# Linear attention and a mixture of adapters in one kernel: filler products moved to listed places, and VectorE adds x for seven groups

## The chip, the cores and the metric

The kernel runs on one NeuronCore of one Trainium2 chip. The metric is the device time of one execution in microseconds. Thirteen executions of the kernel before were timed: median 109.11 us, lowest 107.42, highest 112.18.

Five engines work side by side, each through its own list of instructions in order: TensorE (PE; its weight loads are shown as PEld), VectorE (DVE), ScalarE (ACT), GpSimd (POOL) and SyncE (SP). In this kernel GpSimd and SyncE mostly issue transfers.

## What is computed

Two stages, cut to what matters:

```
r_q, r_k = relu(q), relu(k)                      # 8 batches, 8 heads, 576 rows, 64 columns
q_p = concat(r_q * cos, r_q * sin);  k_p likewise # cos, sin depend on the row
kv  = k_p^T v ;  z = sum over rows of k_p
x   = (q_p kv) / (q_p z + 1e-6)                   # then seen as 4608 rows of 512
logits = x @ w_gate                               # 8 experts
w   = softmax over the two largest logits of a row, zero elsewhere
out = x + sum over experts e of  w[e] * (x @ A[e]) @ B[e]      # A: 512x16, B: 16x512
```

The last line matters here: the output is x plus the adapters' part d.

## The kernel before

**Groups.** The 4608 output rows are 36 groups of 128 rows. The groups of batches 0 to 5 are called by batch and number, (0,0) to (5,8); those of batches 6 and 7 are done in pairs and called (7,0) to (7,8). The chain of one batch is: load k, v and q (cast to bf16 on the way); relu of k (L417); v times cos and sin (`vscale`, L427; VectorE takes 0.67 us for half a batch and 1.27 for a whole one, ScalarE does the same in nine pieces); the products k^T v (`kv_mm`, L439) into a PSUM tile `pnd`; and two copies of those to SBUF as `BD` (`kv_evac`, L454). The chain of one group is: transposes of q (L533) and a relu copy (L539) and the tangent factor (`qt_tan`, L545); the numerator and denominator products (`num_mm`, L562) into a `pnd` tile; a reciprocal (L589) and the division (`x_xt`, L594), which gives x as `xt` in bf16; transposes of x (L603) and their copy; the products with A and the gate (L616); the routing weights on VectorE (L630 to L665); a transpose of the weighted result (L674) and its copy; and last the output products.

**The output products.** For each group `dx_mm` (L682) puts two products of 512 columns in one PSUM bank `ps`: x by the identity matrix (L685), then the weighted result by B on top of it (L687). `osb` (L690) copies the sum to SBUF, on ScalarE (L241) or VectorE (L243), and a store carries it out.

**PSUM.** There are two `pnd` tiles of two banks each (128 x 2 x 512 f32) and four `ps` banks. Of each bank of a `pnd` tile the work uses columns 0 to 259; columns 260 to 511 are unused.

**Fillers.** Eighteen products of a constant tile `warm` open TensorE's list, and eighteen more follow later (`pe_warm`, L298). In addition `pe_more` (L305) puts products of 252 columns into the unused columns of the *first* bank of the `pnd` tile that the step has just written: six behind each of the four half-batch `kv` steps of batches 0 and 1 (L501) and four behind each of the `num` steps of the first five groups (L742), 44 in all:

```
    def pe_more(t, n):
        for _ in range(n):
            nc.tensor.matmul(out=t[:, 0, 4 * W:512], lhsT=warm[:, 0:128], rhs=warm[:, 4 * W:512], ...)
```

W is 65. The reader of a `pnd` tile takes both banks in one instruction, columns 0 to 259 of each, so its address range covers those filler columns of the first bank.

**Order.** All work is 594 steps. `ORDER` (L20) gives the order in which they are emitted, and so the order on each engine; `CHOICE` (L48) says which engine takes a step that has alternatives; `SLOTS` (L66) gives the buffer numbers. The costs and due times in the `pl.add` calls fed the planning that made these lists; nothing is planned when the kernel is built. `HOLD` (L79) makes four stores wait for an earlier issue. Loads go out on GpSimd's queue, the first k through SyncE; each load on GpSimd's queue also waits for the transfer that was issued eight before it. Most stores stand in SyncE's list, the rest behind the loads in GpSimd's.

Of the kernel before, what the change touches and what calls it, by code (L numbers as in the profile page):

```python
# [20 lines left out]
    26, 19, 32, 16, 20, 51, 15, 27, 14, 18, 0, 17, 1, 36, 2, 9, 29, 3, 12, 10, 52, 28, 33, 13, 31, 35, 4, 30, 11, 7,  # L21
    34, 5, 46, 37, 21, 6, 54, 50, 55, 38, 45, 39, 23, 8, 40, 44, 61, 114, 115, 41, 116, 22, 60, 125, 117, 42, 124, 43,
    126, 134, 70, 121, 127, 118, 53, 62, 122, 154, 119, 135, 120, 155, 145, 71, 144, 49, 123, 128, 69, 48, 299, 24,
    156, 131, 129, 47, 130, 298, 136, 132, 301, 133, 56, 146, 137, 79, 65, 302, 300, 57, 25, 78, 303, 58, 59, 355, 64,
    147, 141, 356, 138, 357, 360, 142, 358, 63, 80, 139, 140, 143, 304, 151, 359, 361, 305, 152, 66, 362, 88, 306, 73,
    373, 68, 74, 67, 363, 364, 148, 89, 160, 374, 161, 149, 375, 150, 171, 162, 170, 153, 307, 157, 172, 163, 308,
    376, 378, 164, 309, 158, 173, 87, 181, 159, 200, 377, 180, 201, 191, 165, 379, 166, 190, 182, 167, 380, 311, 192,
    174, 202, 183, 96, 381, 310, 72, 168, 175, 365, 169, 97, 369, 176, 177, 382, 178, 385, 193, 366, 75, 312, 179,
    107, 82, 386, 314, 393, 370, 77, 76, 313, 367, 315, 394, 187, 395, 398, 396, 184, 397, 81, 98, 83, 412, 185, 399,
    188, 186, 316, 189, 194, 400, 317, 203, 195, 413, 106, 196, 216, 217, 414, 417, 368, 197, 204, 415, 318, 416, 218,  # L30
    319, 320, 198, 418, 206, 199, 207, 321, 401, 205, 84, 105, 419, 402, 208, 219, 322, 387, 91, 383, 86, 323, 388,
    430, 209, 85, 392, 405, 384, 92, 210, 324, 420, 213, 211, 421, 406, 246, 403, 431, 247, 212, 226, 372, 227, 404,
    432, 236, 435, 90, 228, 237, 450, 433, 214, 248, 238, 93, 451, 215, 434, 452, 410, 407, 99, 95, 220, 453, 94, 455,
    229, 422, 408, 223, 221, 239, 454, 423, 424, 222, 426, 425, 390, 436, 224, 230, 437, 427, 326, 225, 438, 325, 231,
    439, 328, 456, 232, 329, 327, 233, 457, 444, 234, 330, 101, 429, 458, 440, 240, 459, 441, 235, 469, 445, 241, 446,
    100, 331, 332, 243, 333, 447, 262, 470, 263, 242, 253, 264, 252, 244, 272, 474, 471, 245, 273, 254, 102, 472, 265,
    473, 274, 255, 464, 462, 475, 110, 103, 389, 460, 463, 249, 428, 465, 476, 334, 335, 461, 250, 109, 477, 442, 478,
    466, 283, 336, 282, 487, 251, 443, 108, 479, 284, 337, 448, 488, 111, 275, 338, 492, 489, 285, 480, 483, 113, 411,
    490, 481, 104, 391, 491, 507, 112, 493, 494, 482, 256, 508, 484, 495, 509, 292, 257, 510, 486, 485, 496, 258, 259,
    293, 512, 501, 511, 260, 499, 261, 502, 266, 371, 513, 294, 500, 497, 514, 340, 506, 505, 267, 269, 268, 498, 467,  # L40
    515, 339, 270, 503, 342, 271, 341, 276, 504, 343, 344, 277, 279, 468, 516, 278, 526, 280, 281, 345, 286, 346, 527,
    347, 528, 287, 517, 529, 531, 288, 348, 449, 289, 530, 518, 543, 532, 290, 533, 349, 544, 519, 350, 291, 521, 520,
    548, 534, 545, 295, 546, 522, 535, 524, 523, 351, 547, 296, 538, 549, 352, 525, 550, 536, 409, 539, 297, 540, 537,
    551, 560, 552, 541, 353, 561, 555, 542, 354, 562, 565, 557, 563, 564, 553, 556, 566, 567, 579, 558, 554, 568, 569,
    580, 570, 559, 581, 584, 571, 582, 574, 583, 575, 572, 585, 589, 586, 573, 576, 577, 587, 588, 578, 590, 592, 591,
    593,
]
CHOICE = [  # L48
    0, 0, 0, 0, 0, 0, 0, 0, 0, 0, 0, 0, 0, 0, 0, 0, 0, 0, 0, 0, 0, 0, 0, 0, 0, 1, 0, 0, 0, 0, 0, 0, 0, 0, 0, 1, 0, 0,
    0, 0, 0, 0, 0, 1, 0, 0, 0, 0, 0, 1, 0, 0, 0, 1, 0, 1, 0, 0, 1, 0, 0, 0, 0, 0, 1, 0, 0, 0, 0, 0, 0, 0, 1, 0, 0, 0,  # L50
    0, 1, 0, 0, 0, 0, 0, 1, 0, 0, 0, 0, 0, 0, 0, 0, 0, 0, 0, 0, 0, 0, 0, 0, 0, 0, 0, 0, 1, 0, 0, 0, 0, 0, 0, 0, 0, 0,
# [4 lines left out]
    0, 0, 0, 0, 0, 0, 0, 0, 0, 0, 0, 0, 0, 0, 0, 0, 0, 0, 0, 0, 0, 0, 0, 0, 0, 0, 0, 0, 0, 0, 0, 0, 0, 0, 0, 0, 0, 1,  # L56
    0, 0, 0, 0, 0, 0, 0, 0, 0, 0, 0, 0, 0, 0, 1, 0, 0, 0, 0, 0, 0, 0, 0, 0, 0, 0, 0, 0, 0, 0, 0, 0, 0, 0, 0, 0, 0, 0,
    0, 1, 0, 0, 0, 0, 0, 0, 0, 0, 0, 0, 0, 0, 0, 0, 0, 0, 0, 0, 0, 0, 0, 0, 0, 0, 0, 0, 0, 0, 1, 0, 0, 0, 0, 0, 0, 0,
    0, 0, 1, 0, 0, 0, 0, 0, 0, 0, 1, 0, 1, 0, 0, 0, 0, 0, 0, 0, 0, 0, 0, 0, 0, 0, 1, 0, 0, 0, 1, 0, 0, 0, 0, 0, 0, 0,
    0, 0, 0, 0, 0, 0, 0, 0, 0, 0, 0, 1, 0, 0, 0, 0, 0, 0, 0, 0, 0, 0, 0, 0, 0, 0, 0, 0, 0, 1, 0, 0, 0, 0, 0, 0, 0, 0,  # L60
    0, 0, 0, 0, 0, 0, 0, 0, 0, 0, 0, 0, 0, 0, 0, 0, 0, 0, 0, 0, 0, 0, 0, 0, 0, 0, 0, 0, 0, 0, 1, 0, 0, 0, 0, 0, 0, 0,
    0, 0, 0, 0, 0, 0, 0, 0, 0, 0, 0, 0, 1, 0, 0, 0, 0, 0, 0, 0, 0, 0, 1, 0, 0, 0, 0, 0, 1, 0, 1, 1, 0, 0, 0, 0, 0, 0,
    0, 0, 0, 0, 0, 0, 0, 0, 0, 0, 0, 0, 0, 0, 0, 0, 0, 0, 0, 0, 1, 0, 0, 0, 0, 0, 1, 0, 0, 0, 0, 0, 0, 0, 0, 0, 0, 0,
    0, 0, 0, 1, 0, 0, 1, 1, 0, 0, 0, 0, 0, 0, 0, 0, 0, 0, 1, 0, 0, 0, 0, 0,
]
SLOTS = [  # L66
    2, 1, 0, 3, 0, 1, 0, 0, 0, 0, 0, 0, 1, 1, 1, 1, 0, 1, 2, 2, 2, 2, 1, 2, 3, 3, 3, 0, 0, 3, 0, 0, 4, 1, 0, 0, 1, 1,
    0, 2, 1, 1, 2, 2, 2, 0, 0, 2, 3, 3, 1, 1, 1, 3, 0, 0, 0, 1, 0, 1, 0, 1, 2, 1, 0, 2, 2, 1, 1, 3, 1, 2, 0, 2, 4, 1,
    0, 5, 0, 4, 1, 2, 6, 0, 1, 7, 3, 3, 1, 0, 8, 1, 0, 0, 2, 9, 1, 1, 10, 0, 1, 0, 0, 11, 1, 2, 12, 1, 2, 0, 1, 13, 1,
    0, 14, 3, 3, 0, 2, 15, 0, 0, 0, 0, 4, 1, 1, 2, 2, 1, 1, 2, 4, 0, 0, 1, 0, 0, 0, 1, 5, 1, 2, 3, 3, 4, 0, 0, 7, 1,  # L70
    1, 6, 1, 3, 0, 2, 8, 1, 0, 9, 1, 2, 1, 1, 10, 2, 0, 0, 2, 11, 1, 0, 14, 3, 1, 0, 1, 12, 1, 2, 2, 0, 4, 0, 0, 0, 1,
    1, 15, 0, 3, 0, 2, 13, 1, 0, 4, 1, 2, 0, 1, 5, 2, 0, 3, 1, 0, 2, 3, 3, 0, 0, 2, 1, 2, 2, 1, 3, 1, 0, 3, 1, 1, 2,
    0, 0, 2, 3, 1, 1, 0, 0, 2, 2, 1, 1, 0, 3, 0, 0, 3, 2, 2, 1, 1, 0, 0, 0, 3, 0, 2, 2, 1, 3, 2, 1, 1, 1, 1, 1, 0, 3,
    1, 3, 0, 0, 0, 0, 0, 0, 0, 4, 3, 3, 3, 1, 1, 1, 0, 1, 1, 5, 3, 1, 2, 0, 0, 0, 2, 0, 3, 6, 1, 2, 0, 1, 1, 1, 0, 1,
    0, 0, 2, 3, 1, 0, 0, 0, 3, 1, 2, 1, 1, 0, 3, 1, 1, 1, 3, 0, 1, 5, 3, 0, 2, 0, 0, 0, 3, 1, 3, 3, 3, 2, 2, 1, 1, 1,
    0, 0, 2, 1, 0, 3, 1, 0, 0, 0, 1, 1, 2, 2, 1, 3, 0, 1, 1, 1, 0, 0, 2, 5, 3, 1, 0, 0, 0, 1, 1, 0, 0,
# [3 lines left out]
    (371, 429), (389, 106), (411, 372), (449, 506),  # L80
# [65 lines left out]
def kernel(  # L146
# [86 lines left out]
    def pF(u):  # L233
        return pS[S_(u)][:, :]
# [70 lines left out]
    def pe_more(t, n):  # L305
        for _ in range(n):
            nc.tensor.matmul(out=t[:, 0, 4 * W:512], lhsT=warm[:, 0:128], rhs=warm[:, 4 * W:512], start=True, stop=True,
                             skip_group_check=True)
# [130 lines left out]
    def kv_mm(aa, uk, uvv, up, more=0):  # L439
        def f():  # L440
            kt, vt, pt = tK[S_(uk)], tVV[S_(uvv)], pND[S_(up)]
            for a in aa:
                for j in range(J):
                    for par in range(2):
                        for hh in range(2):
                            r = slice(64 * par, 64 * par + 64)
                            nc.tensor.matmul(  # L447
                                out=pt[64 * hh:64 * hh + 64, par, a * 2 * W:(a + 1) * 2 * W], lhsT=kt[r, 2 * a + hh, j, :],
                                rhs=vt[r, 2 * a + hh, j, :].rearrange("p (c w) -> p c w", c=2)[:, :, 0:W],
                                start=(j == 0), stop=(j == J - 1), skip_group_check=True)  # L450
            pe_more(pt, more)
        return f
# [20 lines left out]
    for b in range(B):  # L473
# [25 lines left out]
        for ai, aa in enumerate([[0], [1]] if b in HALF else [[0, 1]]):  # L499
            more = 6 if b in HALF else 0  # L500
            pl.add("kv", one("PE", 0.02 + 0.58 * len(aa) + 0.105 * more, kv_mm(aa, uk, uvv, upk, more)), d + 9 + ai,  # L501
                   needs=[("k", b, a) for a in aa] + [("vv", b, a, cs) for a in aa for cs in range(2)] + VCOLS,
                   makes=[("kvp", b, a) for a in aa], uses=[uk, uvv, upk, ubd], ins=72 * len(aa) + 2 * more)
# [58 lines left out]
    def num_mm(m, gs, uqt, und, more):  # L562
        g = gs[m]

        def f():
# [15 lines left out]
            pe_more(nd, more)  # L581
# [100 lines left out]
    def dx_mm(udx, uxt, uzt, i, part):  # L682
        def f():
            if part != 1:
                nc.tensor.matmul(out=pF(udx), lhsT=ident, rhs=tXT[S_(uxt)], start=True, stop=False)  # L685
            if part != 0:
# [167 lines left out]
```

## Time and profile before

| | |
|---|---|
| median of 13 executions | 109.11 us (107.42 to 112.18) |
| the profiled execution: its own time | 108.23 us |
| its span from first to last instruction | 106.4 us |
| loads (28.85 MB read from HBM) | end near 72 us |
| last instruction of a compute engine | ends at 102.5 us; then the last store |

| what, on which line | engine | count | from start to the next start, or mean |
|---|---|---|---|
| x by the identity, L685 | TensorE | 36 | 0.215 us |
| d by B, L687 | TensorE | 36 | 0.215 us |
| filler in `pnd`, L307 | TensorE | 44 | 0.107 us |
| numerator of a group, L577 | TensorE | 36 | 0.47 us (8 products), 0.59 (16) |
| division to `xt`, L594 | VectorE | 36 | 0.60 us |
| output copy, L243 / L241 | VectorE / ScalarE | 3 / 30 whole | 0.56 us / 0.50 us |
| reciprocal, L589 | VectorE | 36 | 0.11 us |

How to read the views that are quoted further on. The page's second part cuts the span into 40 slices of 2.66 us; a digit is the busy share of a slice in tenths. A timeline row gives start, duration, engine, line, operation, output and inputs with their size, and how many like instructions are merged; a bracket gives idle time of that engine just before the row and what ended it. A row's duration includes the pipeline's end, which lies beside the next instruction, so the cost of one in a run of them is read from start to start. A windows row gives the stretch, its length, and the busy time and instruction count of each engine in it, then the granted TensorE clock, the DMA share and GB/s.

### The profile page before, as it was taken

How to read it: one execution, taken by the hardware profiler on the slowest of the kernel's cores; microseconds unless marked ns; L12 is line 12 of the kernel's file. 1: busy time of each engine (PE TensorE's matmuls, PEld its weight loads, DVE VectorE, ACT ScalarE, POOL GpSimd, SP SyncE). 2: the span in 40 equal slices, each digit the busy share in tenths (PEclk: the TensorE clock that was granted, in tenths of full speed). 3: DMA queues.
4: the chain of work that ended last, by engine and by line, in shares of the span. 5: the costliest groups of instructions: out<-in, count | busy, mean ns of one | idle time of the engine just before them, and what ended most of it. 6: DMA issues, size and time to landing. Idle time of an engine off the chain costs nothing.

```text
span 106.4 us, 4082 instructions
## 1 busy us (share of the span) xinstructions
PE 94.6 (89%) x1728; PEld 68.7 (65%) x1728; DVE 87.6 (82%) x247; ACT 84.2 (79%) x162; POOL 31.5 (30%) x51
## 2 busy tenths in 40 slices
PE   4999997999759899989899999999999999999710
PEld 1334476888648687668778777796686578765200
DVE  5897306699888999998999889999998988896810
ACT  4539927799699699979999988999999853688720
POOL 5999682545212225222204120120000120040000
PEclk9999999999999999999999999999999999999998
DMA  2999999999999999999999999999998699889992
GB/s 63 387 203 199 191 198 206 206 190 208 207 208 210 212 201 207 208 207 208 208 208 210 207 211 205 208 208 304 377 312 232 153 319 289 271 219 286 428 402 111
DMA packets 18482, 24.71 MB, mean 232 GB/s; under 512 B 4256, under 2 KB 15648, under 8 KB 18464
## 3 DMA queue, kind: packets, MB, share of 16 engines
q0 software_dynamic: 15856, 16.59, 87.0%
q1 hardware_dynamic: 2608, 7.87, 22.6%
q8 instruction: 13, 0.21, 0.7%
q14 instruction: 5, 0.04, 0.1%
HBM read 28.85 MB, written 9.44 MB: 360 GB/s over the span
## 4 chain that ended last, share of the span: by engine, by line
PE 39%; DVE 19%; ACT 15%; DMA 12%; POOL 8%; issue 2%; ACTq 0%; POOLq 0%
ACT VV L434 9%; DMA Kb<-in_k_dram 9%; PE pnd L577 9%; PE ps L616 5%; PE ps L685 5%; PE ps L687 5%; DVE xt L594 5%; PE ps L603 5%; DVE VV L436 5%; PE pnd L447 4%; PE ps L533 4%; POOL Qb L409 4%; DMA out_dram<-osb 3%; DVE qTcs L559 3%; POOL Vb L391 2%
## 5 line engine op out<-in xcount | busy, mean ns | idle before, releaser
L577 PE MATMUL pnd<-BD,qTcs 128*128 128x130 bf16 (+1 forms) x384 | 22.9, 222 | 2.3 <-ACT BD L460 1.4
L594 DVE TENSOR_TENSOR xt<-pnd,rden 128x512 bf16<-128x512 f32 x36 | 24.1, 684 | 0.2
L577 PEld LDWEIGHTS <-qTcs 128*128 128x128 bf16 (+1 forms) x384 | 18.6, 103 | 7.1 <-issue 4.6
L539 ACT ACTIVATE qTcs<-ps 128x1024 bf16<-128x1024 bf16 (+1 forms) x20 | 18.1, 936 | 3.1 <-PE ps L533 1.9
L241 ACT COPY osb<-ps 128x512 f32<-128x512 f32 (+1 forms) x34 | 18.2, 570 | 2.2 <-DVE osb L243 1.0
L241 ACT COPY xT<-ps 128x1024 bf16<-128x1024 bf16 (+1 forms) x18 | 15.9, 898 | 4.3 <-PE ps L603 4.1
L436 DVE TENSOR_TENSOR VV<-Vb,TV 128x2304 bf16<-128x2304 bf16 (+1 forms) x15 | 17.0, 1145 | 0.7 <-DMA Vb<-in_v_dram 0.7
L434 ACT ACTIVATE VV<-Vb,TVf 128x128 bf16<-128x128 bf16 (+1 forms) x45 | 15.6, 432 | 1.7 <-DMA Vb<-in_v_dram 1.7
L559 DVE TENSOR_TENSOR qTcs<-qTcs,TT 128x1024 bf16<-128x1024 bf16 (+1 forms) x20 | 12.3, 624 | 5.1 <-ACT qTcs L539 5.0
L705 POOL DMA_DIRECT2D out_dram<-osb x9 | 4.8, 537 | 37.0 <-ACT osb L241 32.3
L603 PE MATMUL ps<-ident,xt 128*128 128x128 bf16 x144 | 13.2, 221 | 2.0 <-DVE xt L594 1.5
L687 PE MATMUL ps<-Ball,zgT 128*128 128x512 bf16 x36 | 13.7, 379 | 0.5 <-DVE zgT L243 0.3
L685 PE MATMUL ps<-xt,ident 128*128 128x512 bf16 x36 | 13.7, 380 | 0.3 <-DVE zgT L243 0.2
L603 PEld LDWEIGHTS <-xt 128*128 128x128 bf16 x144 | 10.0, 115 | 4.1 <-DVE xt L594 2.3
L301 PE MATMUL ps<-warm 128*128 128x512 bf16 x36 | 10.5, 460 | 1.5 <-DVE warm L295 1.5
L616 PE MATMUL ps<-AW,xT 128*128 128x136 bf16 x144 | 10.7, 223 | 0.4 <-ACT osb L241 0.4
L533 PE MATMUL ps<-ident,Qb 128*64 128x128 bf16 x288 | 10.3, 221 | 0.0
L447 PE MATMUL pnd<-VV,Kb 64*64 64x130 bf16 x576 | 10.3, 218 | 0.0
L616 PEld LDWEIGHTS <-xT 128*128 128x128 bf16 x144 | 8.9, 98 | 1.6 <-issue 0.7
L533 PEld LDWEIGHTS <-Qb 128*64 128x64 bf16 x288 | 8.6, 110 | 2.1 <-issue 1.5
L447 PEld LDWEIGHTS <-Kb 64*64 64x64 bf16 x576 | 8.7, 106 | 1.6 <-issue 0.4
L589 DVE RECIPROCAL rden<-pnd 128x8 f32<-128x8 f32 x36 | 7.1, 202 | 2.5 <-PE pnd L577 1.2
(61 smaller groups left out, 118.7 us busy)
## 6 DMA issues: line engine op xcount, KB each, us to landing
Vb<-in_v_dram POOLq DMA_DIRECT2D x6, 576.0 KB, 19.0
Kb<-in_k_dram POOLq DMA_DIRECT2D x6, 576.0 KB, 20.0
Qb<-in_q_dram POOLq DMA_DIRECT2D x6, 576.0 KB, 20.2
out_dram<-osb SPq DMA_DIRECT2D x11, 256.0 KB, 5.2
out_dram<-osb SPq DMA_DIRECT2D x2, 768.0 KB, 4.5
out_dram<-osb POOLq DMA_DIRECT2D x5, 256.0 KB, 6.0
osb<-in_k_dram SPq DMA_DIRECT2D x2, 576.0 KB, 4.0
Vb<-in_v_dram POOLq DMA_DIRECT2D x4, 288.0 KB, 6.5
```

The lines of the kernel that those rows point to most:

```text
L241: nc.scalar.copy(o, i)
L434: nc.scalar.activation(o[:, :, j], i[:, :, j], AF.Copy, scale=TVf[:, cs, j:j + 1])
L436: nc.vector.tensor_tensor(out=o, in0=i, in1=TV[:, cs].unsqueeze(1).to_broadcast([128, n, J, D]), op=ALU.mult)
L447: nc.tensor.matmul(out=pt[64 * hh:64 * hh + 64, par, a * 2 * W:(a + 1) * 2 * W], lhsT=kt[r, 2 * a + hh, j, :], rhs=vt[r, 2 * a + hh, j, :] ...
L533: nc.tensor.transpose(out=pt[64 * hh:64 * hh + 64, n, 2 * a:2 * a + 2, x], in_=qt[:, c, j, :], identity=ident)
L539: nc.scalar.activation(tQT[S_(uqt)][:, 0, 0:n], pB(up)[:, 0:n], AF.Relu)
L577: nc.tensor.matmul(out=nd[r, a, 0:4 * W].rearrange("p (h e w) -> p h e w", h=2, e=2)[:, :, par], lhsT=st, rhs=bd[:, par, a, cs].rearrange( ...
L594: nc.vector.tensor_tensor(out=tXT[S_(uxt)].rearrange("p (a h d) -> p a h d", a=2, h=4), in0=nd_view(und)[:, :, :, 0:D], in1=tRD[S_(urd)].u ...
L603: nc.tensor.transpose(out=pB(up)[:, lo:lo + 128], in_=tXT[S_(uxt)].rearrange("p (x c) -> p c x", c=4)[:, c], identity=ident)
L616: nc.tensor.matmul(out=pF(uza)[:, n * AW_W:(n + 1) * AW_W], lhsT=tXTT[S_(u)][:, k, c, :], rhs=AW[:, c, :], start=(c == 0), stop=(c == 3))
L685: nc.tensor.matmul(out=pF(udx), lhsT=ident, rhs=tXT[S_(uxt)], start=True, stop=False)
L687: nc.tensor.matmul(out=pF(udx), lhsT=tZGT[S_(uzt)][:, i], rhs=Ball, start=False, stop=True)
```

## The change

Three things are changed together.

1. `pe_more` and its 44 products are gone. `pe_fill` puts 37 products of the same size at six listed places in TensorE's list (`FILL`: the step before which they stand, and how many): 2 before the small table product, 13 before the first numerator (step 118, group (0,0)), 2 before a q transpose (step 135), 10 and 2 before the two `kv` half steps of batch 1 (steps 57 and 56), 8 before the numerator of (1,0) (step 138). They all write the unused columns of the *second* bank of `pnd0`, which lie behind the last column that any reader takes.
2. For groups other than the last three, the output step has a second form: TensorE computes only d (L687's product, with start set), and VectorE adds x from `xt` while it moves the result to SBUF (`osb_add`). It stands in seven groups: (2,1), (2,3), (3,3), (4,0), (4,3), (5,2) and (7,3). `xt` is now held until the output step in all groups.
3. `ORDER`, `CHOICE`, `SLOTS` and `HOLD` are new throughout. Apart from the seven groups, 35 steps change engine or queue; among them, of the twenty `vscale` steps ScalarE has three and not five, VectorE one `kv_evac` and not four, and VectorE the copy of the adapter weights.

The numbers in the diff's lists stand for steps; the lists are cut.

```diff
 HOLD = [
-    (371, 429), (389, 106), (411, 372), (449, 506),
+    (371, 392), (409, 98), (446, 486), (503, 504),
+]
+
+FILL = [
+    (7, 2), (118, 13), (135, 2), (57, 10), (56, 2), (138, 8),
 ]
...
-    def pe_more(t, n):
+    def pe_fill(n):
         for _ in range(n):
-            nc.tensor.matmul(out=t[:, 0, 4 * W:512], lhsT=warm[:, 0:128], rhs=warm[:, 4 * W:512], start=True, stop=True,
+            nc.tensor.matmul(out=pND[0][:, 1, 4 * W:512], lhsT=warm[:, 0:128], rhs=warm[:, 4 * W:512], start=True, stop=True,
                              skip_group_check=True)
...
-    def dx_mm(udx, uxt, uzt, i, part):
-        def f():
-            if part != 1:
+    def dx_mm(udx, uxt, uzt, i, parts):
+        def f():
+            if "x" in parts:
                 nc.tensor.matmul(out=pF(udx), lhsT=ident, rhs=tXT[S_(uxt)], start=True, stop=False)
-            if part != 0:
-                nc.tensor.matmul(out=pF(udx), lhsT=tZGT[S_(uzt)][:, i], rhs=Ball, start=False, stop=True)
+            if "d" in parts:
+                nc.tensor.matmul(out=pF(udx), lhsT=tZGT[S_(uzt)][:, i], rhs=Ball, start=parts == "d", stop=True)
         return f
...
+    def osb_add(udx, uxt, uo, i):
+        def f():
+            nc.vector.tensor_tensor(out=tOSB[S_(uo)][:, i], in0=pF(udx), in1=tXT[S_(uxt)], op=ALU.add)
+        return f
...
-                pl.add("dx", one("PE", 0.44, dx_mm(udx, uxt, uzt, i, 2)), dd + 6 + i, needs=[("zgT", key), "Ball"],
+                pl.add("dx", [("PE", 0.44, dx_mm(udx, uxt, uzt, i, "xd")), ("PE", 0.22, dx_mm(udx, uxt, uzt, i, "d"))], dd + 6 + i, needs=[("zgT", key), "Ball"],
                        makes=[("dx", g)], uses=[uxt, uzt, udx], extra=0.12, ins=4)
-                pl.add("osb", [("ACT", 0.5, osb(udx, uo, i, "ACT")), ("DVE", 0.6, osb(udx, uo, i, "DVE"))], dd + 6.4 + i,
-                       needs=[("dx", g)], makes=[("osb", g)], uses=[udx, uo])
+                pl.add("osb", [("ACT", 0.5, osb(udx, uo, i, "ACT")), ("DVE", 0.6, osb_add(udx, uxt, uo, i))], dd + 6.4 + i,
+                       needs=[("dx", g)], makes=[("osb", g)], uses=[uxt, udx, uo])
...
         hold, issued = dict(HOLD), {}
+        fill = dict(FILL)
         for s in order:
+            if s.idx in fill:
+                pe_fill(fill[s.idx])
             issued[s.idx] = s.emit()
```

(In the new form VectorE's alternative of the output step is always the add with the short product.) In the built program's instruction order TensorE has 14 products and 14 weight loads fewer, VectorE three instructions more and ScalarE eleven rows fewer. The waits that the build puts on the fillers can be read there too: the first of the 13 waits for ScalarE's copy out of `pnd0` that precedes it, the first of the 10 for the division of group (0,2) out of `pnd0`, and the first of the 8 for ScalarE's copy of batch 1 out of `pnd0`.

Early in GpSimd's list the order becomes: row numbers for the tables (`TVi`, now first), pieces 4 and 5 of q of batch 0, a half of v of batch 1, the gate weights, both halves of v of batch 0, its pieces 0 and 1, and only then the identity matrix (`ident`, before third). The loads up to the last half of k of batch 1 are the same ones in another order, and the later ones are exchanged with their neighbours only.

## The prediction

> **What bounds the kernel now.** I read the page's busy shares, then its slices, then windows cut at four events, then the timelines of VectorE and TensorE around those events.
>
> ```profile
> PE 94.6 (89%) x1728; PEld 68.7 (65%) x1728; DVE 87.6 (82%) x247; ACT 84.2 (79%) x162; POOL 31.5 (30%) x51
> DVE  5897306699888999998999889999998988896810
> PEclk9999999999999999999999999999999999999998
> GB/s 63 387 203 199 191 198 206 206 190 208 207 208 210 212 201 207 208 207 208 208 208 210 207 211 205 208 208 304 377 312 232 153 319 289 271 219 286 428 402 111
> ```
>
> No engine is the bound by its share. The GB/s row is flat at about 207 from slice 3 to 27: loads stream without a pause until 72 us (27 slices of 2.66 us), at one rate, so a load lands when the bytes before it are through, and later than that only if its issue waits. VectorE's row has its only large hole in slices 5 and 6 (10.6 to 16 us).
>
> ```profile
> core 0: us, PE busy (x) PEld busy (x) DVE busy (x) ACT busy (x) POOL busy (x), PEclk, DMA share, GB/s
> 16.27:29.14 12.87, 11.38 (x231) 9.83 (x230) 10.98 (x24) 10.51 (x21) 5.64 (x8) 1.00 1.30 203
> 29.14:77.73 48.59, 45.45 (x998) 36.41 (x996) 46.70 (x126) 45.39 (x79) 9.98 (x16) 1.00 1.20 224
> 77.73:95.25 17.52, 17.43 (x333) 12.75 (x331) 15.68 (x59) 12.70 (x26) 2.04 (x4) 1.00 0.85 256
> 95.25:106.40 11.15, 5.52 (x38) 2.63 (x36) 4.91 (x20) 5.47 (x14) 0.14 (x1) 0.95 0.83 302
> ```
>
> The cuts are the first tangent product, the first reciprocal of batch 1, the last relu of k, and the last division. In the second stretch VectorE is busy 46.70 of 48.59 us: it is the bound there, with 1.89 us idle. In the third TensorE is (17.43 of 17.52). The last is a chain of latencies and the last stores.
>
> ```profile
> 16.27 0.69 DVE L559 TENSOR_TENSOR qTcs<-qTcs,TT 128x1024 bf16<-128x1024 bf16 x1 [4.70 <-ACT qTcs L539]
> 19.09 0.21 DVE L589 RECIPROCAL rden<-pnd 128x8 f32<-128x8 f32 x1 [0.16 <-PE pnd L307]
> 19.99 0.21 DVE L589 RECIPROCAL rden<-pnd 128x8 f32<-128x8 f32 x1 [0.69 <-PE pnd L307]
> 29.14 0.21 DVE L589 RECIPROCAL rden<-pnd 128x8 f32<-128x8 f32 x1 [0.23 <-PE pnd L577]
> 32.30 0.18 DVE L660 TENSOR_TENSOR w<-ps,sig 128x24 f32<-128x24 f32 x1 [0.66 <-ACT sig L655]
> 61.55 0.32 DVE L630 MAX8 m<-ps 128x8 f32<-128x8 f32 x3 [0.63 <-PE ps L616]
> 95.25 0.68 DVE L594 TENSOR_TENSOR xt<-pnd,rden 128x512 bf16<-128x512 f32 x1
> ```
>
> Brackets are waits: 4.70 us for the first group's q, then 0.16 and 0.69 us for fillers (L307) that a reciprocal needed not have waited for, and later only short ones.
>
> ```profile
> 18.00 0.63 PE L577 MATMUL pnd<-BD,qTcs 128*128 128x130 bf16 x8 [0.64 <-DVE BD L462]
> 18.46 0.59 PE L307 MATMUL pnd<-warm 128*128 128x252 bf16 x4
> 78.70 1.24 PE L447 MATMUL pnd<-VV,Kb 64*64 64x130 bf16 x72
> 93.78 0.66 PE L577 MATMUL pnd<-BD,qTcs 128*64 128x130 bf16 x16
> 98.68 0.40 PE L616 MATMUL ps<-AW,xT 128*128 128x136 bf16 x4 [0.41 <-ACT osb L241]
> ```
>
> The last `kv` starts at 78.70, right after the last relu, with no wait of its own; the last numerator follows 15.1 us later.
>
> **The change, stage by stage.** Costs are from start to start, against the profiled execution: 108.23 us, span 106.4.
>
> *Front, to the first reciprocal of batch 1.* Loads first: the same bytes stand ahead of the last half of k of batch 1, so it still lands at 19.3 us, where ScalarE's relu of it starts now (row of 19.32). Placing v of batch 0 by bytes (0.29 MB a half, 1.4 us at 207 GB/s, behind the early k that ends at 5.2 us) puts its last half at 10.9 us; the identity, behind seven GpSimd issues (0.6 to 1.34 us each), at 7.5 us against 3.4 now. I walk on from there with the rows' times. The tangent table's input ends at 8.4 us, the small table product follows, the 18 warm products (3.9 us) end at 12.6 (now 13.1). Half a `kv` (0.65), two q transposes (0.56), the large table product (1.0), the second half (0.65): 15.5. ScalarE's copy out of `pnd0` ends at 16.1. The 13 fillers wait for that copy, though nothing reads what they write, and hold the first numerator behind them: 13 x 0.107 = 1.4, to 17.55, against 18.00 now. VectorE meanwhile does two `vscale` halves in what is a hole now, so no wait of theirs counts. The reciprocals come at 18.6 without the 0.16 and 0.69 us, the divisions end at 20.05 (now 21.4). Then division of (0,2) at 23.1, ten fillers behind it (1.07), `kv` of batch 1 with two more (0.2) to 25.9, two ScalarE copies (1.2), eight fillers (0.86), the numerator (0.5): reciprocal at 28.6, against 29.14. VectorE's own work to that point would allow 27.0, which gives a gain of 2.2; q or the identity late by as much as the 13 fillers last (1.4) gives a loss of 0.9. I take **-0.5**, the walk, as all its steps have rows.
>
> *Second stretch, VectorE to the last relu of k.* Counting both lists: VectorE gains two copies with add (three adds against one copy; an add has no row, its nearest is the division, same size and one f32 PSUM source: 0.60; bounds are the copy's 0.56 and the division's whole duration, 0.68, which move the three by -0.1 and +0.2), the adapter weights' copy (0.6 from ScalarE's 0.63 and 0.23), two routing maxima (0.23 each), a sum and a mask (0.17); it loses a BD copy (0.65) and an xT copy (0.60). 1.2 + 0.6 + 0.46 + 0.17 - 0.65 - 0.60 = **+1.2**. Here VectorE is the bound and the whole of it counts. The three x products that TensorE saves (3 x 0.215) lie beside it and are worth nothing. Idle time on VectorE I leave at 1.89: ScalarE, which ends the 0.66 us wait, is freer, two `vscale` of 3.6 us fewer less two relus; but adds bring new waits for TensorE. Bounds: 0 idle (-1.9), twice as much (+1.9).
>
> *Third stretch, TensorE from the last `kv`.* Four x products go ((4,0), (4,3), (5,2), (7,3)): 4 x 0.215 = 0.86; the q transpose of (7,8) now stands earlier: 0.25. **-1.1**. VectorE has 0.4 more here (two adds and one xT copy in, BD copy, maximum and zgT copy out) beside 1.84 us of idle. If VectorE takes over, the gain is 0 at worst.
>
> *Last stretch.* In the row of 98.68 the last gate product starts 2.1 us after its transposes (96.56), held by a ScalarE output copy out of its bank. In the new list TensorE has five output products and a transpose there (5 x 0.215 + 0.17 = 1.25), while the copy that frees the bank follows the first two by 0.5 and fits beside: 2.1 - 1.25 = **-0.8**. Bounds: 0, if a store's landing holds the copy as one now does for 0.17 us, to -1.7, if the last two routing chains also overlap.
>
> Stores: 9.4 MB after 72 us need 24 us at 400 GB/s (slices 38 and 39); 30 are there. Queue waits on GpSimd (12 stores, now 10) lie behind the last load. Holding `xt` to the output step costs nothing while 16 buffers turn over. The fillers that go from batches 0 and 1 (44 x 0.107 = 4.7) lie in the front and are in its walk.
>
> Sum: -0.5 + 1.2 - 1.1 - 0.8 = -1.2, so 107.0 in the profiled execution's time. That execution is 0.8% under the median (108.23 against 109.11): 107.0 x 109.11 / 108.23 = **107.9 us**.
>
> [...] The rows: the opening warm products start 0.427 us apart until 6.1 us and 0.216 after, half the clock; afterwards the clock row has no dip until the last slice, and TensorE's longest wait is 1.1 us. [...] By the rows alone a gap left open might cost half the clock for as long as it took to come at the start, 4.7 us, worth 2.3 us. [...]
>
> **Rivals.**
> - *The front runs clear* (-2.2 for -0.5) with the rest as forecast: -2.9, 106.2 us. For it: VectorE's hole is filled and ScalarE freed. Against: three filler blocks stand behind copies out of `pnd0`.
> - *Nothing comes of it*: third and last stretch give only what VectorE's 1.2 takes: 109.1 us. For it: VectorE has 3.6 us more in all (seven adds, three fewer other copies) and is nearly as full as TensorE in the third stretch.
> - *VectorE waits for the short products* (slower). Its list is in order; an add that comes before its d product is through stops divisions and routing behind it. Price: the waits now ended by TensorE are 0.23 to 0.63 us, mean 0.43; 7 x 0.43 = 3.0, less 1.2: +1.8, 110.0 x 1.008 = 111.0 us. It cancels the gain from 0.17 us per add (1.2 / 7), and makes it over 1% slower from 0.33. For it: six of the seven adds have a wait on TensorE in the build. Against: ScalarE's copies, which wait alike, show short ones now.
>
> **How the numbers follow.** Forecast 0.42, the front clear 0.16, nothing 0.20, waiting adds 0.22. About 1% is what a measurement of this kernel can tell from no change: 108.0 to 110.2 us is "same". The forecast's own range is 106.8 to 109.0, and 0.27 of its 0.42 lies under 108.0. Faster: 0.27 + 0.15 = 0.42. Slower: 0.20 + 0.02 = 0.22. Same: 0.36. The range reaches from the clear front with part of a last stretch of -1.7 (105.4) to the waiting adds (111.0).
>
> **What would show it.** Right: first numerator near 17.5 us, first reciprocal of batch 1 near 28.6, last relu of k near 78.4, last `kv` to last numerator 14.0 us instead of 15.1, last output copy near 101.3. Wrong: waits of VectorE for L687's successor before adds (0.33 us and more each), fillers still running after VectorE is ready for a reciprocal, a clock row under 9 in slices 5 to 12, or a load that starts late because its buffer is not free (a dip in GB/s before slice 28).

## The result, and the profile after

The changed kernel took 110.77 us (median of 11 executions, 110.28 to 112.31), against 109.03 us before (48 executions, 107.42 to 112.18). The ratio is **1.0218, 95% interval 1.0188 to 1.0248**: 2.2% slower. The value lies near the upper end of the predicted range (105.4 to 111.0), slower where 107.9, faster, was forecast.

The profiled execution took 112.31 us, span 110.2, the longest of the eleven, so its lines show where time goes and the ratio shows how much. All ratios here leave out slow executions (over 1.5% above the fastest of the same kernel): this profiled one is among them, and so are one of 374 and one of 178 us, the profiled ones of two experiments (the first without fillers, and the one with only the 13 moved), whose profiles are not read. From the page of the changed kernel, the busy shares, VectorE's slices, the granted clock and the loads:

```profile
PE 95.8 (87%) x1714; PEld 69.1 (63%) x1714; DVE 90.1 (82%) x254; ACT 77.6 (70%) x139; POOL 32.7 (30%) x53
DVE  6971817189779999997999898998899999989940
PEclk9999997699999999999999999999999999999999
GB/s 73 361 167 193 193 199 206 207 207 195 205 207 209 207 208 208 207 207 209 209 206 210 206 208 210 205 241 394 298 184 251 209 249 290 262 138 266 326 391 144
```

As the two profiles count, VectorE runs 7 instructions more than before (254 against 247), not three, and ScalarE 23 fewer (139 against 162). VectorE has holes in slices 4, 6 and 8, the last of them where before had none (19 to 22 us), and PEclk is under 9 in slices 7 and 8 (16.5 to 22 us). The loads still stream at about 207 GB/s to slice 26. Cut at the same four events as before, the stretches are:

```profile
core 0: us, PE busy (x) PEld busy (x) DVE busy (x) ACT busy (x) POOL busy (x), PEclk, DMA share, GB/s
16.61:32.48 15.87, 12.97 (x223) 10.62 (x223) 11.16 (x21) 7.36 (x9) 6.10 (x9) 0.89 1.28 204
32.48:83.78 51.30, 47.57 (x1016) 37.64 (x1014) 48.05 (x137) 45.28 (x74) 10.71 (x17) 1.00 1.15 224
83.78:100.10 16.32, 15.94 (x318) 11.96 (x316) 15.40 (x57) 10.98 (x23) 2.18 (x4) 1.00 0.85 235
100.10:110.20 10.10, 4.85 (x36) 2.31 (x33) 5.61 (x23) 3.96 (x10) 0.00 (x0) 0.98 0.72 281
```

The first reciprocal of batch 1 comes 3.3 us later than before (forecast: 0.5 earlier), the second stretch takes 2.7 us more (forecast 1.2 more), the third 1.2 less (1.1 less), the last 1.05 less (0.8 less). The front and the second stretch are what has to be explained. VectorE's and ScalarE's rows at the places that the prediction named:

```profile
15.99 0.69 DVE L465 CAST BD<-pnd 64x520 bf16<-64x520 f32 x1 [2.57 <-PE pnd L451]
16.72 0.60 ACT L463 CAST BD<-pnd 64x520 bf16<-64x520 f32 x1 [0.80 <-DVE BD L465]
21.61 0.28 DVE L590 RECIPROCAL rden<-pnd 128x8 f32<-128x8 f32 x2 [3.00 <-PE pnd L579]
32.48 0.21 DVE L590 RECIPROCAL rden<-pnd 128x8 f32<-128x8 f32 x1 [0.50 <-PE pnd L579]
50.83 0.21 DVE L590 RECIPROCAL rden<-pnd 128x8 f32<-128x8 f32 x1 [0.74 <-PE pnd L579]
77.56 0.28 DVE L590 RECIPROCAL rden<-pnd 128x8 f32<-128x8 f32 x2 [0.85 <-PE pnd L579]
```

The two copies out of `pnd0` run one after the other, and VectorE then stands idle for 3.00 us until the first numerators are there. TensorE's rows show what they waited for:

```profile
17.37 2.67 PE L311 MATMUL pnd<-warm 128*128 128x252 bf16 x13 [1.43 <-ACT BD L463]
19.83 1.68 PE L579 MATMUL pnd<-BD,qTcs 128*128 128x130 bf16 x16
26.55 1.24 PE L311 MATMUL pnd<-warm 128*128 128x252 bf16 x10 [1.18 <-DVE xt L595]
30.95 1.02 PE L311 MATMUL pnd<-warm 128*128 128x252 bf16 x8 [0.97 <-ACT BD L463]
50.52 0.75 PE L579 MATMUL pnd<-BD,qTcs 128*128 128x130 bf16 x10 [0.86 <-issue]
76.69 0.36 PE L604 MATMUL ps<-ident,xt 128*128 128x128 bf16 x3 [0.52 <-issue]
84.57 1.24 PE L451 MATMUL pnd<-VV,Kb 64*64 64x130 bf16 x72 [0.30 <-DVE Kb L428]
98.03 0.66 PE L579 MATMUL pnd<-BD,qTcs 128*64 128x130 bf16 x16
```

Three blocks of fillers start only after a wait of 1.43, 1.18 and 0.97 us and then stand between the end of that wait and the work that needed the tile. The 13 took 2.46 us from start to start, not 1.4, and the two numerators behind them 1.61, where they take 1.03 at full clock in other runs: that is half the clock. The same rows show two pauses "issue" inside groups of equal products, 0.86 and 0.52 us (a third, of 0.23 us, stands at 56.38). In them TensorE waits for nothing that the profile shows; VectorE's two longest waits of the second stretch, 0.74 and 0.85 us, follow them. Cut at the clock's own steps (columns as above), TensorE had these two stretches:

```profile
14.23:17.64 3.41, 1.98 (x43) 1.12 (x42) 1.65 (x3) 2.29 (x5) 2.21 (x4) 1.00 1.34 202
17.64:21.05 3.41, 3.41 (x24) 2.78 (x23) 0.98 (x2) 0.00 (x0) 1.67 (x4) 0.50 1.21 204
```

This fall of the clock is not in the 2.2%. One step of 3.41 us at half clock alone brings the mean granted clock of an execution to 0.985 or less (1 - 0.5 x 3.41 / 110.2). The mean is 0.983 here and 0.981 in one other execution of the changed kernel (112.00 us), at least 0.986 in all the rest, and the ratio leaves out just these two.

### The profile page after: what moved, and what is told of

Read it like the earlier page. It is cut to its first block, busy times and chain, and to the rows that moved or that the text cites. A ratio compares the mean times of both kernels' runs of the same rounds, so it can differ in the third digit from the quotient of the medians.

```text
span 110.2 us, 4050 instructions
## 1 busy us (share of the span) xinstructions
PE 95.8 (87%) x1714; PEld 69.1 (63%) x1714; DVE 90.1 (82%) x254; ACT 77.6 (70%) x139; POOL 32.7 (30%) x53
## 4 chain that ended last, share of the span: by engine, by line
PE 58%; DVE 20%; ACT 14%; issue 4%; DVEq 0%
PE pnd L579 12%; PE ps L305 10%; PE pnd L451 7%; PE pnd L311 5%; DVE xt L595 5%; PE ps L604 5%; PE ps L688 4%; PE ps L535 4%; PE ps L617 4%; ACT qTcs L541 4%; ACT BD L463 4%; PE ps L686 4%; ACT VV L438 3%; DVE VV L440 3%; DVE qTcs L561 2%
## 5 line engine op out<-in xcount | busy, mean ns | idle before, releaser
L440 DVE TENSOR_TENSOR VV<-Vb,TV 128x2304 bf16<-128x2304 bf16 (+1 forms) x17 | 18.9, 1139 | 2.3 <-DMA Vb<-in_v_dram 2.3
L245 ACT COPY xT<-ps 128x1024 bf16<-128x1024 bf16 (+1 forms) x16 | 14.9, 942 | 4.5 <-PE ps L604 4.3
L245 ACT COPY osb<-ps 128x512 f32<-128x512 f32 (+1 forms) x29 | 15.6, 568 | 3.4 <-PE ps L688 1.7
L604 PE MATMUL ps<-ident,xt 128*128 128x128 bf16 x144 | 13.8, 222 | 0.9 <-issue 0.5
L688 PE MATMUL ps<-Ball,zgT 128*128 128x512 bf16 x36 | 13.2, 380 | 0.6 <-DVE zgT L247 0.6
L305 PE MATMUL ps<-warm 128*128 128x512 bf16 x36 | 11.0, 476 | 1.5 <-DVE warm L299 1.5
L535 PE MATMUL ps<-ident,Qb 128*64 128x128 bf16 x288 | 11.1, 221 | 0.4 <-DVE zg L666 0.3
L463 ACT CAST BD<-pnd 64x520 bf16<-64x520 f32 x15 | 9.0, 598 | 3.3 <-PE pnd L451 2.3
L686 PE MATMUL ps<-xt,ident 128*128 128x512 bf16 x29 | 10.9, 381 | 0.3 <-DVE zgT L247 0.3
```

What stands on the lines that cost most here:

```text
L245: nc.scalar.copy(o, i)
L305: nc.tensor.matmul(out=pF(up), lhsT=warm[:, 0:128], rhs=warm, start=True, stop=True)
L440: nc.vector.tensor_tensor(out=o, in0=i, in1=TV[:, cs].unsqueeze(1).to_broadcast([128, n, J, D]), op=ALU.mult)
L535: nc.tensor.transpose(out=pt[64 * hh:64 * hh + 64, n, 2 * a:2 * a + 2, x], in_=qt[:, c, j, :], identity=ident)
L604: nc.tensor.transpose(out=pB(up)[:, lo:lo + 128], in_=tXT[S_(uxt)].rearrange("p (x c) -> p c x", c=4)[:, c], identity=ident)
L688: nc.tensor.matmul(out=pF(udx), lhsT=tZGT[S_(uzt)][:, i], rhs=Ball, start=parts == "d", stop=True)
```

## The experiments

Ratios are to the kernel before on the same chip, with 95% intervals. In the expectations, theory A is the fillers' places and the clock, B is VectorE's work, C the new lists by themselves.

**The change again** (nothing edited).

> The changed kernel once more, nothing edited, on the same chip as the next three. Theory A (the front: the 13 fillers stand behind the copies out of pnd0 and the clock falls to half at 17.6 us): the first numerator again near 19.8 us and a stretch of half clock again. Theory B (VectorE's extra work, in the stretch where it is the bound): VectorE busy about 48.05 us from the first reciprocal of batch 1 to the last relu of k again. Theory C (the new lists by themselves: loads, waits and TensorE's three pauses of 0.86, 0.23 and 0.52 us inside groups of equal products, where it waited for nothing that the profile shows): the three pauses again at the same instructions. All three: 110.8 us.

Measured: 1.0199 (1.0131 to 1.0267), median 111.35. The profiled execution has the first numerator at 19.83 us, half the clock from 17.69 to 21.10 us and the three pauses at the same instructions. The picture repeats; this one too is one of two with a mean clock under 0.985 (of six).

**The fillers in the tile that nobody holds.** Nothing else is changed.

```diff
-    (7, 2), (118, 13), (135, 2), (57, 10), (56, 2), (138, 8),
+    (7, 2, 0), (118, 13, 1), (135, 2, 0), (57, 10, 1), (56, 2, 1), (138, 8, 1),
...
-    def pe_fill(n):
+    def pe_fill(n, x):
...
-            nc.tensor.matmul(out=pND[0][:, 1, 4 * W:512], ...
+            nc.tensor.matmul(out=pND[x][:, 1, 4 * W:512], ...
```

> The changed kernel with the 13, 10, 2 and 8 fillers in the unused columns of pnd1, which no unfinished reader holds at these places; the two blocks of 2 at steps 7 and 135 stay in pnd0. Theory A: the 13 run in the gap of 1.43 us, the clock stays at 1.00, the first numerator starts at 17.4 to 17.6 us, the first reciprocal of batch 1 near 29.5 us for 32.5, in all 107.8 us. Theory B or C: at least 109.5 us, as the time goes elsewhere.

Measured: **0.9985** (0.9944 to 1.0027), median 108.95. With the same 37 products no longer behind a copy the kernel takes 2.3% less: all of the loss is gone. TensorE's rows there:

```profile
15.60 1.57 PE L311 MATMUL pnd<-warm 128*128 128x252 bf16 x13
17.10 1.10 PE L579 MATMUL pnd<-BD,qTcs 128*128 128x130 bf16 x16
```

The 13 now run in the gap, without a bracket, the numerators follow at 17.10 us, and the first reciprocal of batch 1 comes at 28.65 us. Theory A had 29.5 for it and 107.8 us in all. The front gave more than that, but the total stayed at 108.95; a pause of 1.75 us in the third stretch took part of it back in this execution.

**Only the 13 moved** ((118, 13, 1), the others in `pnd0`).

> The changed kernel with only the 13 fillers moved to pnd1, so that they wait for nothing; the others as they are. If the 13 are the cost: first numerator near 17.2 us, first reciprocal of batch 1 near 29.2 us (30.6 in the run without adds, whose clock held, less the 13's 1.4), in all 109.0 to 109.5 us. If the blocks of 10 and 8 cost as much: 110.0 us or more.

Measured: 1.0037 (0.9978 to 1.0095), median 109.70. The 13 are about 1.8 of the 2.3%. The half per cent that is left to the other moved blocks is within the two intervals, and with no profile to read, the times expected inside this run stay unchecked.

**No fillers at all** (`FILL` empty), run twice.

> The changed kernel without any of the 37 fillers. Theory A by the place of the fillers alone (clock holds): first numerator at 17.4 us, kv of batch 1 1.1 us earlier, numerator of (1,0) 0.86 us earlier again, first reciprocal of batch 1 near 29.2 us for 32.5, in all 107.5 us. Theory A by the clock (gaps left open cost half the clock in two more stretches of 3.4 us, 1.7 us each): 109.2 to 111. Theories B and C: the front comes earlier but the second stretch keeps its 51.3 us, 108.5 to 109.5 us.

> The changed kernel without any of the 37 fillers once more, for its profile. If only the fillers' places cost the time, the clock row is 1.00 up to the last slices, the first numerator starts near 17.2 us and the first reciprocal of batch 1 near 28.6 us. If open gaps cost half the clock, a stretch of half clock of 3.4 us or more stands between 14 and 32 us and the first reciprocal of batch 1 comes 1.7 us later per such stretch. 108.4 us either way, as before.

Measured: 0.9949 (0.9904 to 0.9993), median 108.39, and 0.9963 (0.9912 to 1.0014), median 108.46. In the second profile the first numerator starts at 17.19 us after the same wait of 1.43 us, the first reciprocal of batch 1 comes at 28.28 us, and the granted clock is 1.00 from 4.63 to 103.62 us:

```profile
17.19 1.10 PE L578 MATMUL pnd<-BD,qTcs 128*128 128x130 bf16 x16 [1.43 <-ACT BD L462]
87.58 0.28 PE L578 MATMUL pnd<-BD,qTcs 128*64 128x130 bf16 x3 [1.12 <-issue]
```

So in this list the fillers bought nothing in that execution, and the open gap by itself did not cost the clock. That it never does is not shown: two other executions of the second run have mean clocks of 0.956 and 0.969, and no profile.

**The kernel before without its fillers** (`pe_more` puts none).

> The kernel before without its 44 fillers. If fillers only stand in the way: its readers' waits on them (0.16, 0.69 and 0.37 us) go, 107.7 to 108.4 us for 108.8. If fillers keep the clock: stretches of 3.4 us at half clock between 14 and 32 us, 1.7 us each, 109.5 to 110.5 us.

Measured: **1.0249** (1.0178 to 1.032), median 112.52, mean granted clock 0.949 to 0.982 over its six executions. Without them the clock falls here. The windows, cut at the clock's steps:

```profile
25.13:28.54 3.41, 1.08 (x16) 1.05 (x17) 3.38 (x9) 2.60 (x6) 1.51 (x3) 1.00 1.21 207
28.54:31.95 3.41, 2.31 (x24) 2.04 (x22) 2.64 (x8) 3.41 (x10) 0.99 (x2) 0.50 1.21 208
31.95:35.37 3.42, 3.42 (x86) 3.05 (x85) 2.83 (x5) 1.29 (x4) 1.04 (x2) 0.50 1.22 210
```

After 3.41 us with TensorE busy for 1.08, the clock is halved for two steps of 3.41 us and comes back after one in which TensorE never stopped. TensorE's longest idle gap before the fall was 2.10 us. Two pauses "issue" of 0.97 and 2.13 us in the second stretch add to this profile's time, so the 2.5% is not the clock's alone.

**No adds in the changed kernel** (seven groups in the first form; fillers as in the change).

> The changed kernel with the seven groups in the first form again: both products on TensorE and ScalarE's copy (7 x 0.60 us off VectorE, 7 x 0.215 on TensorE, 7 x 0.50 on ScalarE). Theory A or C: no gain, as only two of the seven adds lie before the last relu of k: 110.3 to 111.8 us. Theory B (VectorE's adds cost the time): 1.2 us faster for the two in its stretch, up to 3 us with the other five: 107.8 to 109.6 us.

Measured: 1.0304 (1.0241 to 1.0367), median 112.32: about 1% slower than with the adds, so B falls. (The profiled execution, 111.25 us, is the shortest of its six, so its rows do not show where that 1% goes.) (Three adds, not two, lie before the last relu of k: at 71.54, 73.75 and 80.04 us.) This run also has the front of the change without the fall of the clock:

```profile
17.12 1.56 PE L311 MATMUL pnd<-warm 128*128 128x252 bf16 x13 [1.43 <-ACT BD L463]
18.51 1.10 PE L579 MATMUL pnd<-BD,qTcs 128*128 128x130 bf16 x16
15.62:19.03 3.41, 1.98 (x28) 1.87 (x23) 2.63 (x4) 0.64 (x2) 1.70 (x3) 1.00 1.32 204
19.03:22.44 3.41, 3.41 (x77) 2.73 (x75) 2.26 (x6) 2.13 (x3) 1.48 (x2) 1.00 1.21 207
```

The gap and the 13 fillers are the same, TensorE was busy for the same 1.98 us of a step, and yet the next step has the full clock. The first reciprocal of batch 1 comes at 30.58 us. So of the 3.9 us by which the change's profile missed the prediction's 28.6, 1.9 are the halved clock (32.48 against 30.58). The other 2.0 are a miss of the walk itself, which had the fillers at these places in it. What the places cost is 30.58 against 28.65, 1.9 us.

**Adds alone in the kernel before** (the second form in the same seven groups, everything else as before).

> The kernel before with nothing but the second form of the output step in the same seven groups (VectorE adds x, TensorE leaves the x product out). If the adds are worth what undoing them cost in the changed kernel (1.0 %): 107.8 us for 108.8. If VectorE, the bound of the second stretch, pays for three adds of 0.60 us there and TensorE gains 4 x 0.215 us in the third: 0.9 us slower, 109.7 us.

Measured: 1.0152 (1.0094 to 1.0209), median 110.24. The second and the third stretch:

```profile
28.93:79.30 50.37, 45.38 (x995) 36.32 (x993) 48.49 (x129) 43.84 (x76) 10.17 (x16) 1.00 1.19 227
79.30:96.76 17.46, 17.12 (x331) 12.53 (x329) 16.88 (x61) 11.22 (x24) 1.98 (x4) 1.00 0.77 228
```

VectorE is busy for 1.79 us more in the second and the stretch is 1.78 us longer: 0.59 us for each of three adds, the price that the prediction took from the division's row. In the third VectorE fills up (16.88 of 17.46) and TensorE's four shorter steps bring 0.06 us.

**Fillers that wait for nothing, and adds in one stretch only.** Base: blocks of 13, 10 and 8 in `pnd1`, none of 2. Then the three adds before the last relu of k undone, or the four behind it.

> The changed kernel with the blocks of 13, 10 and 8 fillers in pnd1, where they wait for nothing unfinished, and without the three blocks of 2 (one of which waited 0.47 us for a division). If the fillers that stand in the way are the whole loss of the front: first numerator near 17.1 us, first reciprocal of batch 1 near 28.2 us, clock row 1.00, in all 108.2 to 108.8 us against 109.0 for the kernel before. If the clock needs the blocks of 2 as well: a stretch at half clock before 32 us and 109.5 us.

> As the run with fillers that wait for nothing, and the three adds that lie before the last relu of k undone ((2,1), (2,3), (3,3): both products on TensorE, ScalarE's copy). If VectorE's work sets the second stretch, as in the kernel before with adds (+1.8 us for three): 1.8 us faster than that run, near 106.7 us. If ScalarE and TensorE have no room for what comes back, as the run without any add suggested: 0 to 1.7 us slower, 108.5 to 110.2 us.

> As the run with fillers that wait for nothing, and the four adds that lie behind the last relu of k undone ((4,0), (4,3), (5,2), (7,3)). If TensorE's 4 x 0.215 us are worth their length in the third stretch: 0.9 us slower than that run, near 109.4 us. If they are worth nothing there, as in the kernel before with adds (third stretch 0.06 us shorter): within 0.3 us of it.

Measured: base 0.999 (0.995 to 1.003), without the early adds 0.9982 (0.9947 to 1.0016), without the late ones 1.0048 (1.0017 to 1.0079). The base has 28.75 us to the first reciprocal of batch 1, and stretches of 50.49, 16.53 and 10.12 us. The late adds are worth about 0.4 us (109.04 against 108.61), between the two numbers expected, and the intervals overlap. The early ones are worth nothing either way: without them VectorE's work in the second stretch falls by 1.2 us (46.83 against 48.00), yet the stretch is longer (51.63), as VectorE then waits more, the longest for ScalarE's sigmoid and for the gate products:

```profile
68.22 0.18 DVE L661 TENSOR_TENSOR w<-ps,sig 128x24 f32<-128x24 f32 x1 [0.81 <-ACT sig L656]
79.17 0.32 DVE L631 MAX8 m<-ps 128x8 f32<-128x8 f32 x3 [1.08 <-PE ps L617]
```

Neither number expected for the early ones came out.

**39 products more, as long in all.** The pauses "issue" inside equal products stood near the same product numbers (of the first product behind the pause, counted from 0) in the profiles of the change's list, though not all of them in each. The kernel before had none. The trace's record of transfers has pieces of 16,384 bytes on the instruction queue, and the start of the next product (the end of the pause) follows the start of such a piece by:

```
run                    product number: end of pause, time since the last piece began
changed kernel         733: 50.52, 2.36     861: 56.38, 2.21    1244: 76.69, 2.29
fillers in pnd1        733: 45.90, 2.32    1499: 86.34, 2.17
before, no fillers     863: 57.64, 2.37    1246: 78.18, 2.55
no late adds           733: 46.12, 2.35     861: 52.22, 2.42    1239: 72.48, 2.30   1491: 86.70, 2.20
```

To tell a place in the instruction stream from the work that stands there, 52 fillers of 63 columns replaced the 13 of 252.

> As the run with fillers that wait for nothing, but with 52 products of 63 columns in place of the 13 of 252: as long in all (1.4 us), 39 products more. If TensorE's pauses come from the supply of instructions (pieces of 128 products): they stay near the product numbers 733, 861 and 1239, so 39 products earlier in the work, and may change in length by 1 us either way. If they belong to the work: 0.47 us at number 772 and 0.27 us at 1278, inside the same numerators. Otherwise the same time, 108.6 us, and the first numerator at 17.1 us.

> The run with fillers that wait for nothing once more, as partner on the same chip: 108.6 us; pauses of TensorE again near the product numbers 733 and 1239, 0.2 to 0.6 us each.

Measured: 1.0082 (1.0032 to 1.0132) and, for the partner, 1.0025 (0.9979 to 1.007). The partner paused at numbers 733, 861, 1244 and 1499 for 0.60, 0.20, 0.27 and 1.67 us. With 39 products more the pause is again at number 733, which is now inside a `kv` and not a numerator:

```profile
44.09 0.31 PE L452 MATMUL pnd<-VV,Kb 64*64 64x130 bf16 x8 [0.86 <-issue]
```

It ends 2.35 us after a piece began. The pause at 1499, too, stands at that number with 37 fillers (1.75 us), with 31 (1.67) and with none (1.12). So the pauses stand at a place in the instruction stream, 2.2 to 2.6 us behind the start of a piece, and not at a place in the work. What was not foreseen is that the other three are gone in this run, and that it is none the less 0.6% slower than its partner; the intervals overlap, and no cause is shown.

**The version that the runs point to**: no fillers and the three early adds undone.

> The changed kernel without fillers and with the three adds before the last relu of k undone: the two edits that were not slower, together. If both hold: 0.994 to 0.997 of the kernel before, 108.1 to 108.5 us where that stands at 108.8, with the first numerator near 17.2 us. If the open gaps cost the clock in this list, as in the kernel before without fillers: a stretch at half clock before 32 us and 110 us or more.

Measured: **0.9934** (0.989 to 0.9979), median 108.16 against 109.69 for the kernel before, granted clock 1.00 to 104.5 us, no pause "issue" over 0.15 us. It is 0.7% faster than the kernel before, little but clear of its interval, and so faster than the changed one. That undoing the adds adds anything to leaving out the fillers (0.9949 and 0.9963) is not shown.

## Why the prediction was wrong

*Front, -0.5 forecast, +3.3 in the profile.* This is the step that failed. The walk let ScalarE's copy out of `pnd0` end at 16.1 us, 0.6 behind the products, as if it ran beside VectorE's. It waits for VectorE's and ends at 17.3 (17.06 in the run without adds, whose clock held). Before's rows have the two copies one after the other as well, whichever comes first, and were not read for it:

```profile
16.61 0.60 ACT L460 CAST BD<-pnd 64x520 bf16<-64x520 f32 x1 [0.37 <-PE pnd L307]
17.24 0.70 DVE L462 CAST BD<-pnd 64x520 bf16<-64x520 f32 x1 [0.28 <-ACT BD L460]
27.83 0.60 ACT L460 CAST BD<-pnd 64x520 bf16<-64x520 f32 x1 [0.88 <-DVE BD L462]
```

The 13 fillers and the first numerator stand behind the later copy, so that with the clock held the numerator starts at 18.51 us and not at 17.55. That is half of the walk's miss of 2.0 us (30.58 against 28.6). The other half gathered further on, where the division of (0,2) ended 1.5 us late and `kv` of batch 1 1.8; it was not taken apart. With the fillers out of the way 28.65 and 28.75 us were measured. That this is the walk's own number is chance, as the walk had 3.5 us of fillers in its path (1.4, 1.07, 0.2 and 0.86).

The fall of the clock is a second miss, of the profile alone. The price of a gap was left outside the sum because no trace had a gap without fillers; but the walk itself put an unfilled gap, the wait for that copy, ahead of the 13, and the fall after it cost 1.9 us more in this execution. Without it the four stretches add up to +1.9 us (1.44 + 2.71 - 1.20 - 1.05), near the 2.4 us that 2.2% are.

*Second stretch, +1.2 forecast, +2.7.* VectorE's work was sized right: 48.05 against 46.70 us, +1.35. The idle time, which the sum left at 1.89, became 3.25: this is the term that was mis-sized. TensorE's pauses make 1.61 us in this stretch. Less its pauses it is 49.69 us, and 49.56, 49.75, 50.07, 50.43 and 50.57 in the five profiles of the list with all adds whose fillers do not wait or are gone: 1.4 over before in the mean of the six. So the pauses, which the prediction did not know of, fit the rest of the miss to some tenths; no run took them away and left all else alone. The prediction's "it is the bound there" does not hold for the new list: undoing three adds did not shorten the stretch.

*Third, -1.1 forecast, -1.2*, and -1.0 in the list with free fillers, which had no pause there. Right. The late adds' part was measured at 0.4 us end to end against 0.86 of products.

*Last, -0.8 forecast, -1.05.* Right in size by luck, not in cause: from the last division to the last output copy 0.27 us went (7.27 to 7.00), the store behind it gave 0.8 (3.9 to 3.1).

*The rivals.* "VectorE waits for the short products" ended on the right side for a wrong reason: no add in the profile has a wait ahead of it. What was named at the end as showing the prediction wrong, fillers that run after VectorE is ready (3.00 us) and a clock row under 9 in slices 5 to 12, is what came. "The front runs clear" did not come even in the list without fillers (28.28 us, 0.9 earlier than before, for 2.2).

*The fillers and the clock.* The clock fell after gaps of 1.43 us (the change) and 2.10 us (before without fillers), and held after the same 1.43 us in the profiles without adds and without fillers. That the fillers of the change are loss alone is what the runs without them showed for its list (0.9949 and 0.9963 of the kernel before, against 1.0218 with them); in the kernel before, leaving them out cost 2.5%, part of it the clock.

## What to carry to other kernels

With the fillers of the change, three blocks of which waited for readers of `pnd0`, the kernel took 1.0218 of the time before; with these in a tile that nobody held 0.9985, and with none 0.9949 and 0.9963. So before placing a filler, read in the build what its first instruction waits for, and put it ahead of the wait it is to fill, not behind it. When a step is walked by hand, look up in the old trace whether two neighbours on different engines really run side by side. A change of emission order also moves other work to the places in the instruction stream at which TensorE paused here (numbers 733, 861 and 1499), and such pauses differ between executions of one kernel (0.74 us in all in one profile of the free fillers, 2.74 in the other), so compare several executions before putting a difference of 1 us down to the work. And look at the mean clock of every execution before explaining a median by the profile of one.

## What the runs showed of the hardware

- In these profiles the granted clock changed after 3.41 us or a multiple of it: half for 3.41 us in the change and 6.83 in before without fillers, full for 10.24 and 88.75 us (3 and 26 times 3.413) in the change. The same wait of 1.43 us was followed by a fall in both profiles of the change, and by none in the profiles without adds, without fillers and of the last version. What in a step decides is not settled: 1.98 us of products in one were followed by half the clock in the change and by the full clock in the run without adds. The products differed (in the first case mostly the table product and small `kv` ones, in the second fillers and numerators), and no run here separated that.
- TensorE paused at places in the instruction stream: the pauses of 0.20 to 2.13 us in the table above and in the run with 39 products more ended 2.2 to 2.6 us after a piece of 16,384 bytes on the instruction queue began to move, at product numbers that lie about a multiple of 128 apart (733, 861, 1239 to 1246, 1491 to 1499). That TensorE had no instruction left in them is a reading of these times, which no record shows directly; why some pieces are followed by a pause and others are not stays open.
